# A top-k attention and two expert layers on one core: the order of all instructions settled with other costs and latencies

## The chip, the cores and the metric

The kernel runs on one core of a Trainium2 chip. The metric is the device time of one execution in microseconds (us), taken as the median of repeated runs. Five instruction streams work side by side: TensorE (PE, with its weight loads shown apart as PEld), VectorE (DVE), ScalarE (ACT), GpSimd (POOL) and SyncE (SP), which here issues every DMA.

## What is computed

```python
scores = scale * np.matmul(q, k.transpose(0, 1, 3, 2))          # 4 batches, 8 heads, 576 x 576, head size 64
kth = np.partition(scores, -top_k, axis=-1)[..., -top_k:-top_k + 1]   # top_k = 32
scores = np.where(scores >= kth, scores, -1000000000.0)
scores = scores - np.max(scores, axis=-1, keepdims=True)
attn = np.exp(scores)
attn = attn / (np.sum(attn, axis=-1, keepdims=True) + 1e-09)
x = np.matmul(attn, v)                                          # regrouped to 2304 tokens x 512
h = x @ w_in                                                    # 512 x 2048
x = (h * (1.0 / (1.0 + np.exp(-1.702 * h)))) @ w_out            # 2048 x 512
a = x @ w1; b = x @ w2                                          # 512 x 1024 each
out = ((a * b) @ w3) @ w4                                       # 1024 x 1024, 1024 x 512
```

The weights come as 64-bit floats, q, k and v as 32-bit ones.

## The kernel before

**Numbers.** A 32-bit operand is split into two 16-bit ones, a rounded upper part ("hi") and the rest ("lo"); a product is three matmuls: hi by hi, hi by lo, lo by hi (lines 488, 489, 490, in `product_op`). w3 and w4 are multiplied with each other once ("w34"), so that each token tile needs four products: "h" (w_in), "x2" (w_out), "a" and "b" (w1, w2), "o" (w34). The four weight stores are called win, wout, w12 and w34. While the weights are prepared, free ones of them serve as staging, so the trace shows names such as w<-wout.

**Weight stage.** `load64` brings 128 x 512 numbers of 64 bits by DMA (line 356), three or four passes over ScalarE and GpSimd make pieces of a float (lines 361, 366 or 371, 375), and VectorE joins them (line 379). There are 72 such blocks. A sum of squares over TensorE (line 406) gives one scale for a weight, and `split_op` makes hi and lo of it: hi at lines 313, 330 or 316, lo at 323 (VectorE) or 326 and 327 (GpSimd).

**Attention.** There are 18 tiles of 128 rows, each with 8 heads: 144 heads in all. `head` issues for one of them: S on TensorE (line 706, four or eight matmuls of 128x288); the 32 greatest of 576 on VectorE, four times MAX8 (line 728) with three MATCH_REPLACE8 between (line 731); a bias nb (line 738, GpSimd or VectorE); two passes on ScalarE (746, 749); hi on ScalarE (755), lo on GpSimd (758, 759); a transpose by DMA (762, SP); and the product with v, "av", on TensorE (769, nine or eighteen matmuls). The scores of only two heads fit in PSUM (s_ps).

**Expert layers.** `tile_end` gathers a tile of 8 heads (lines 809, 813, 838), scales it, splits it and transposes it (851). `moe` runs the four products with their splits and transposes between (921 for g, 958 for x2, 1025 for p, the store at 1041). A transposed operand lies in tsb, the operand before in hsb, of which there are three buffers.

**What sets the order.** Nothing is issued as the code is read. Every operation is handed to a planner, class `Order`: with the engines that may take it and a cost in us on each, a due time as priority, the operations it waits for, and the buffers it takes and gives back. `run` then steps through a modelled time. Whenever an engine (T, V, A, G for TensorE, VectorE, ScalarE, GpSimd; D for SP's queue) is free, it takes the ready operation of lowest due time whose buffers are free. An operation becomes ready when the last one it waits for has ended plus a gap: SAME for the same engine, GAP for another. A DMA keeps D for its cost and ends DMA us after that. The order in which operations are taken is the order of instructions on each engine; an operation with several engines goes to the one that takes it first. The chip sees no modelled time, only the order and the semaphores. The due times are set at each call; TensorE's attention work has due - 1000, so that S and av go ahead of products.

```python
u.ready = max(u.ready, o.end + (self.SAME[o.eng] if same else self.GAP))
...
o.end = now + a[1] + (self.DMA if e == "D" else 0.0)
```

Of the kernel before, what the change touches and what calls it, by code (L numbers as in the profile page):

```python
# [35 lines left out]
class Order:  # L36
# [3 lines left out]

    GAP = 0.25
    SAME = {"T": 0.0, "V": 0.11, "A": 0.12, "G": 0.1, "D": 0.25}
    DMA = 2.3

# [7 lines left out]

    def op(self, alts, due, deps=(), env=None, acq=(), rel=(), tag=""):
        o = Op()
        o.alts, o.prio = alts, due
        o.acq = [(a, env, a) if isinstance(a, str) else a for a in acq]
        o.rel = [(a, env, a) if isinstance(a, str) else a for a in rel]
        o.left, o.users, o.ready, o.end, o.why = 0, [], 0.0, None, None
        o.tag, o.seq, o.done = tag, len(self.ops), False
        for d in deps:  # L60
            if d is not None:
                d.users.append(o)
                o.left += 1
        self.ops.append(o)
        return o

    def run(self, log=None):
# [12 lines left out]
        while n < len(self.ops):  # L80
# [18 lines left out]
            for e in engs:  # L99
# [62 lines left out]
def kernel(  # L162
# [126 lines left out]
    def dve_chain(due, fns, deps=(), env=None, acq=(), rel=(), tag=""):  # L289

        o = None
        for i, f in enumerate(fns):
            first, last = i == 0, i == len(fns) - 1
            o = dve(
                0.09, due, f, deps=deps if first else [o], env=env, acq=acq if first else [], rel=rel if last else [], tag=tag
            )
        return o
# [7 lines left out]
    def dma(cost, due, fn, **kw):  # L305
        return op([("D", cost, fn, 0.0)], due, **kw)

    def split_op(due, hi, lo, src, sc, n, deps, env, rel, acq=(), tag="", lo_dve=2.0):
# [22 lines left out]

        o = op([("A", 0.09 + 0.52 * k, f_hi, 0.0), ("G", 0.12 + 0.57 * k, f_hi_g, HI_G), ("V", 0.1 + 0.6 * k, f_hi_v, lo_dve)], due, deps=deps, env=env, acq=acq, tag=tag + "hi")
# [15 lines left out]
    def load64(dst, src, raw_pool, deps):  # L348
# [33 lines left out]

        ld = dma(1.5, due - 20, f_load, deps=deps, env=E, acq=[raw_pool], tag="w load")
        lo = act(0.69, due, f_low, deps=[ld], tag="w low")
        sg = op([("A", 0.55, f_sign_a, 0.0), ("G", 0.9, f_sign, SIGN_G)], due, deps=[lo], tag="w sign")
# [89 lines left out]
    def transpose_op(due, src, acq, dep, env, n=8):  # L475
        def f():
            nc.sync.dma_start_transpose(out=env[acq], in_=src())

        return dma(1.0, due, f, deps=[dep], env=env, acq=[acq], rel=["h"], tag="T")

# [113 lines left out]
    def kv_prep(b, hp, is_v):  # L594
# [53 lines left out]

        kready[b, hp] = [dma(2.0, due, f_t, deps=[m, r], env=E, acq=["kt"], rel=["h", "kr"], tag="k T")]

# [3 lines left out]
    def q_prep(t):  # L654
# [31 lines left out]
        if t == 0:  # L686
            start_prep.append(m)
        tr = dma(1.0, due, f_t, deps=[m], env=E, acq=[("q", E, "qa")], rel=["h"], tag="q T")
        qready[t] = [dma(1.3, due, f_swap, deps=[tr], env=E, acq=[("q", E, "qb")], tag="q swap")]


    def head(t, h, X):
# [87 lines left out]
        if first and j == 0:  # L780
            X["esc", hp] = pool(1.1 * len(pt), due - 6, f_esc(hp, hp + 1), deps=[s], tag="esc")
        elif h == 0:
            o = pool(1.1 * len(pt), due - 6, f_esc(0, NPAIR), deps=[s] + [d for b, _, _, _ in pt for i in range(NPAIR) for d in kready[b, i]], tag="esc")
# [7 lines left out]
        nb = op(  # L791
            [("G", 0.41, f_nb(nc.gpsimd), 0.0), ("V", 0.18, f_nb(nc.vector), NB_DVE)], due - 6, deps=[d, X["esc", hp]],
            env=E, acq=["nb"], tag="nb",
        )
# [24 lines left out]
    def tile_end(t, X):  # L819
# [49 lines left out]
        )  # L869
        X["xt"] = dma(1.0, due, f_t, deps=[s], env=X, acq=["t"], rel=["h"], tag="x T")  # L870


    def hi_lo(due, E, src, deps, rel, acq=(), tag="", wait=2.0, wait_hi=2.0):
# [11 lines left out]
        a = op([("A", 0.52, h_a, 0.0), ("V", 0.42, h_v, wait_hi)], due, deps=deps, env=E, acq=["h"], tag=tag + "hi")  # L885
        return op([("G", 1.18, l(nc.gpsimd), 0.0), ("V", 0.68, l(nc.vector), wait)], due, deps=[a], env=E, rel=rel, tag=tag + "lo")

    def moe(t, X):
# [9 lines left out]
        for j in range(NG):  # L898
# [122 lines left out]
        for j in range(NP_):  # L1021
# [75 lines left out]
```

## Time and profile before

| | us |
|---|---|
| median of three runs (lowest, highest) | 1158.55 (1156.67, 1162.78) |
| the profiled execution, its device time | 1158.71 |
| its span, first to last instruction | 1156.9 |

| engine | busy us | share of the span | instructions |
|---|---|---|---|
| PE | 950.6 | 82% | 5654 |
| DVE | 960.4 | 83% | 2112 |
| ACT | 824.5 | 71% | 1555 |
| POOL | 847.8 | 73% | 1142 |

The profile is of one execution. An engine counts as busy from an instruction's start to its end; consecutive instructions overlap a little, and a matmul's end is modelled, so a busy share is an upper bound of what is used. A wait row names who waited, whom for, and for how long in total. The rows that the prediction uses stand in a section of their own below.

### The profile page before, as it was taken

To read this page: it belongs to the slowest core of one execution; us is meant where nothing else is said; L and a number is where in the kernel's file an instruction comes from. 1 tells how busy PE (TensorE), PEld (TensorE's weight loads), DVE (VectorE), ACT (ScalarE), POOL (GpSimd) and SP (SyncE) were. 2 spreads that over 40 slices of the span, in tenths; PEclk is the share of its full clock that TensorE was granted. 3 is DMA by queue.
4 is the path that set the end of the run, shared out by engine and by line. 5 is a ranking of instruction groups with operands and counts; after the bars stand their busy time and mean duration, and the time that the engine had idled before them with its cause. 6 is when DMAs were issued, how large, how long until landed. Compare 5 with 4: busy or idle time off the path is not lost. (4 is left out here: it accounts for less than half of the span.)

```text
span 1156.9 us, 18481 instructions
## 1 busy us (share of the span) xinstructions
PE 950.6 (82%) x5654; PEld 493.7 (43%) x5654; DVE 960.4 (83%) x2112; ACT 824.5 (71%) x1555; POOL 847.8 (73%) x1142
## 2 busy tenths in 40 slices
PE   2335784556869899999889998989999999999996
PEld 1223342323435445544444544544455455555442
DVE  4887795998999888889898898899999999997311
ACT  6977769768777776877678776767868787776421
POOL 4987796657778878878688886858798787686320
PEclk9999996676979999999899998989999999999998
DMA  8959968466835846677668756666765756657331
GB/s 245 299 134 245 218 163 222 114 150 162 172 56 119 149 103 127 118 143 127 122 116 154 124 113 129 118 110 123 128 136 109 146 110 131 112 96 117 71 59 36
DMA packets 428739, 156.95 MB, mean 136 GB/s; under 512 B 406624, under 2 KB 414816, under 8 KB 428640
## 3 DMA queue, kind: packets, MB, share of 16 engines
q1 hardware_dynamic: 428640, 155.78, 65.0%
q8 instruction: 44, 0.72, 0.3%
q14 instruction: 55, 0.45, 0.1%
HBM read 52.43 MB, written 4.72 MB: 49 GB/s over the span
## 5 line engine op out<-in xcount | busy, mean ns | idle before, releaser
L728 DVE MAX8 m8s<-wsb 128x8 f32<-128x576 f32 x432 | 323.5, 754 | 5.4
L731 DVE MATCH_REPLACE8 wsb<-m8s,wsb 128x576 f32<-128x576 f32 x288 | 213.7, 742 | 0.0
L488 PE MATMUL mm<-w,tsb 128*128 128x512 f16 x432 | 167.9, 389 | 16.4 <-DMA tsb<-hsb 16.3
L488 PEld LDWEIGHTS <-tsb 128*128 128x128 f16 x1072 | 106.5, 99 | 156.6 <-DMA tsb<-hsb 47.1
L759 POOL TENSOR_TENSOR hlb<-ysb,hlb 128x512 f16<-128x512 f32 x144 | 168.1, 1168 | 0.0
L489 PE MATMUL mm<-w,tsb 128*128 128x512 f16 x432 | 167.4, 387 | 0.0
L490 PE MATMUL mm<-w,tsb 128*128 128x512 f16 x432 | 166.7, 386 | 0.0
L490 PEld LDWEIGHTS <-tsb 128*128 128x128 f16 x1072 | 106.7, 100 | 132.6 <-issue 10.6
L769 PE MATMUL av<-v2s,ats 128*128 128x130 f16 (+1 forms) x1440 | 114.1, 235 | 49.5 <-DMA ats<-hlb 40.4
L489 PEld LDWEIGHTS <-tsb 128*128 128x128 f16 x1072 | 106.6, 99 | 110.9 <-issue 13.1
L488 PE MATMUL mm<-wout,tsb 128*128 128x512 f16 x352 | 136.1, 387 | 19.7 <-DMA tsb<-hsb 16.7
L728 DVE MAX8 m8s<-s_ps 128x8 f32<-128x576 f32 x144 | 108.8, 756 | 47.4 <-PE s_ps L706 38.9
L746 ACT ACTIVATE s_ps<-s_ps,m8s 128x576 f32<-128x576 f32 x144 | 102.4, 711 | 54.7 <-DVE m8s L728 45.8
L749 ACT ACTIVATE ysb<-s_ps,nbs,asm 128x576 f32<-128x576 f32 x144 | 119.6, 831 | 28.3 <-DVE nbs L738 13.5
L490 PE MATMUL mm<-wout,tsb 128*128 128x512 f16 x352 | 136.0, 386 | 0.0
L489 PE MATMUL mm<-wout,tsb 128*128 128x512 f16 x352 | 135.9, 386 | 0.0
L769 PEld LDWEIGHTS <-ats 128*128 128x128 f16 (+1 forms) x1440 | 97.3, 108 | 82.9 <-DMA ats<-hlb 53.2
L706 PE MATMUL s_ps<-kts,qts 128*128 128x288 f16 (+1 forms) x640 | 106.8, 312 | 30.8 <-ACT ysb L749 24.7
L488 PE MATMUL mm<-win,tsb 128*128 128x512 f16 x288 | 112.4, 390 | 5.6 <-DMA tsb<-hsb 3.1
L489 PE MATMUL mm<-win,tsb 128*128 128x512 f16 x288 | 112.0, 389 | 0.0
L490 PE MATMUL mm<-win,tsb 128*128 128x512 f16 x288 | 111.8, 388 | 0.0
L918 POOL TENSOR_TENSOR fsb<-fsb 128x512 f32<-128x512 f32 x68 | 88.2, 1298 | 29.4 <-ACT fsb L909 27.1
(194 smaller groups left out, 1877.4 us busy)
## 6 DMA issues: line engine op xcount, KB each, us to landing
w<-in_moe_w_dram SPq DMA_DIRECT2D x16, 512.0 KB, 5.3
wout<-in_moe_w_in_dram SPq DMA_DIRECT2D x16, 512.0 KB, 5.3
wout<-in_moe_w_out_dram SPq DMA_DIRECT2D x16, 512.0 KB, 4.7
qts<-qts SPq DMA_DIRECT2D x36, 128.0 KB, 2.6
out_dram<-fsb SPq DMA_DIRECT2D x18, 256.0 KB, 2.4
w<-in_moe_w_out_dram SPq DMA_DIRECT2D x8, 512.0 KB, 5.0
psb<-in_moe_w_dram SPq DMA_DIRECT2D x8, 512.0 KB, 4.6
tsb<-in_moe_w_dram SPq DMA_DIRECT2D x8, 512.0 KB, 5.1
```

Of the source, the lines that this page charges most:

```text
L488: nc.tensor.matmul(o, a[:, i, :], hi, start=(first and i == 0), stop=False)
L489: nc.tensor.matmul(o, a[:, i, :], lo, start=False, stop=False)
L490: nc.tensor.matmul(o, a[:, 4 + i, :], hi, start=False, stop=(last and i == 3))
L706: nc.tensor.matmul(E["sp"][r : r + n, i], qe[q_][:, h, r : r + n], kt[:, j, i * HS : (i + 1) * HS], start=k_ == 0, stop=k_ == 1,)
L728: nc.vector.max(out=E["m8"][:, 8 * i : 8 * i + 8], in_=E["sp"] if i == 0 else E["w"])
L731: nc.vector.match_replace(out=two(E["w"]) if i == 0 else E["w"], in_to_replace=E["m8"][:, 8 * i : 8 * i + 8], in_values=E["sp"] if i == 0 ...
L746: nc.scalar.activation(E["sp"], E["sp"], AF.Prelu, bias=E["m8"][:, TOPK - 1 : TOPK], scale=-1.0, alpha=1.0 / FAR)
L749: nc.scalar.activation(two(E["y"]), E["sp"], AF.Exp, bias=E["nb"], scale=nesc)
L759: nc.gpsimd.tensor_tensor(hl()[:, S + SR : 2 * S], E["y"][:, 0:SM], hl()[:, 0:SM], op=ALU.subtract)
L769: nc.tensor.matmul(X["av", hp][r : r + n, j], E["at"][:, i, r : r + n], v2[:, j, blk, :], start=(i == 0), stop=(i == 8))
L918: nc.gpsimd.tensor_tensor(E["f"], E["f"], E["f2"], op=ALU.mult)
```

## The change

Only the numbers that the planner works with are changed; no operation is added or taken away, and no due time. The one gap of 0.25 us to another engine becomes five, by the engine that ends. A DMA's time after its issue becomes 2.1 us for all and can be set for one operation (`lat`); the weight loads have 3.6. A transpose's time on SP goes from 1.0 (1.1 for a head's) to 1.32 (1.35), the three transposes of a k operand together from 2.0 to 3.9. Some thirty costs of operations are set anew, most by under 0.2 us. The diff, cut to these:

```diff
-    GAP = 0.25
+    GAP = {"T": 0.25, "V": 0.16, "A": 0.16, "G": 0.1, "D": 0.05}
     SAME = {"T": 0.0, "V": 0.11, "A": 0.12, "G": 0.1, "D": 0.25}
-    DMA = 2.3
+    DMA = 2.1
...
-                    u.ready = max(u.ready, o.end + (self.SAME[o.eng] if same else self.GAP))
+                    u.ready = max(u.ready, o.end + (self.SAME[o.eng] if same else self.GAP[o.eng]))
...
-                o.end = now + a[1] + (self.DMA if e == "D" else 0.0)
+                o.end = now + a[1] + ((self.DMA if o.lat is None else o.lat) if e == "D" else 0.0)
                 for name, env, key in o.rel:
-                    t = o.end + self.GAP
+                    t = o.end + self.GAP[e]
...
-        alts = [("V", 0.1 + 0.9 * k, f_lo_v, lo_dve)]
+        alts = [("V", 0.1 + (1.0 if tag == "w " else 0.6) * k, f_lo_v, lo_dve)]
         if lo_dve > 0.0:
-            alts.append(("G", 0.4 + 1.5 * k, f_lo_g, 0.0))
+            alts.append(("G", 0.5 + (2.0 if tag == "w " else 1.4) * k, f_lo_g, 0.0))
...
-        ld = dma(1.5, due - 20, f_load, deps=deps, env=E, acq=[raw_pool], tag="w load")
+        ld = dma(1.3, due - 20, f_load, deps=deps, env=E, acq=[raw_pool], tag="w load", lat=3.6)
...
-        return dve(0.87, due, f_join, deps=[sg, mn], env=E, rel=[raw_pool], tag="w join")
+        return dve(0.72, due, f_join, deps=[sg, mn], env=E, rel=[raw_pool], tag="w join")
...
-        kready[b, hp] = [dma(2.0, due, f_t, deps=[m, r], env=E, acq=["kt"], rel=["h", "kr"], tag="k T")]
+        kready[b, hp] = [dma(3.9, due, f_t, deps=[m, r], env=E, acq=["kt"], rel=["h", "kr"], tag="k T")]
...
-        lo = pool(1.5, due + 7, f_lo, deps=[hi], env=E, rel=["y"], tag="a lo")
-        tr = dma(1.1, due + 8, f_t, deps=[lo], env=E, acq=["at"], rel=["hl"], tag="a T")
+        lo = pool(1.42, due + 7, f_lo, deps=[hi], env=E, rel=["y"], tag="a lo")
+        tr = dma(1.35, due + 8, f_t, deps=[lo], env=E, acq=["at"], rel=["hl"], tag="a T")
...
-            gs.append((E, dma(1.0, due, f_t, deps=[lo], env=E, acq=["t"], rel=["h"], tag="g T")))
+            gs.append((E, dma(1.32, due, f_t, deps=[lo], env=E, acq=["t"], rel=["h"], tag="g T")))
```

**Two places in the new order.** On VectorE, in the weight stage, where blocks of w_out are joined (L379: the staging buffers lie in wout, the store is w_70, that is w12; L728 and L731 are attention). Before:

```order
L379 SCALAR_TENSOR_TENSOR w_70<-wout,w_70 128x512
L728 MAX m8s<-wsb 128x8
L738 TENSOR_SCALAR nbs<-m8s,asm 128x1
L379 SCALAR_TENSOR_TENSOR w_70<-wout,w_70 128x512 x3
L728 MAX m8s<-s_ps_95 128x8
L731 MATCH_REPLACE wsb<-m8s,s_ps_95 128x576
L379 SCALAR_TENSOR_TENSOR w_70<-wout,w_70 128x512
L728 MAX m8s<-wsb 128x8
L731 MATCH_REPLACE wsb<-m8s,wsb 128x576
L379 SCALAR_TENSOR_TENSOR w_70<-wout,w_70 128x512
L728 MAX m8s<-wsb 128x8
L731 MATCH_REPLACE wsb<-m8s,wsb 128x576
```

With the change:

```order
L379 SCALAR_TENSOR_TENSOR w_70<-wout,w_70 128x512
L728 MAX m8s<-wsb 128x8
L728 MAX m8s<-s_ps_95 128x8
L731 MATCH_REPLACE wsb<-m8s,s_ps_95 128x576
L728 MAX m8s<-wsb 128x8
L379 SCALAR_TENSOR_TENSOR w_70<-wout,w_70 128x512
L731 MATCH_REPLACE wsb<-m8s,wsb 128x576
L728 MAX m8s<-wsb 128x8
L731 MATCH_REPLACE wsb<-m8s,wsb 128x576
L379 SCALAR_TENSOR_TENSOR w_70<-wout,w_70 128x512 x2
L813 TENSOR_TENSOR xsb<-xsb,av 128x2x64
L728 MAX m8s<-wsb 128x8
```

Six joins with seven attention instructions became four joins with eight. Counted over the whole stage, the last of the 72 joins stands behind 97 MAX8 (24.25 heads) before and behind 113 (28.25 heads) with the change; the 40th behind 40 and 43.

On SP, at the end, the transposes of the last tile's attention output (L851) and of the next to last tile's g (L921); L762 is the last head's. Before:

```order
L762 DMA_TRANSPOSE ats<-hlb 128x9x128
L1025 DMA_TRANSPOSE tsb<-hsb 128x8x128 x2
L921 DMA_TRANSPOSE tsb<-hsb 128x8x128
L851 DMA_TRANSPOSE tsb<-hsb 128x8x128
L921 DMA_TRANSPOSE tsb<-hsb 128x8x128
L1041 DMA out_dram<-fsb 128x512
```

And with the change:

```order
L762 DMA_TRANSPOSE ats<-hlb 128x9x128 x2
L1025 DMA_TRANSPOSE tsb<-hsb 128x8x128 x2
L851 DMA_TRANSPOSE tsb<-hsb 128x8x128
L921 DMA_TRANSPOSE tsb<-hsb 128x8x128 x2
L1041 DMA out_dram<-fsb 128x512
```

The last tile's transpose has moved ahead of both of the g transposes.

## Rows read from the trace of the kernel before

**Rows 1.** Busy time by stage: us, then PE, PEld, DVE, ACT, POOL; PEclk, DMA share, GB/s.
```profile
0.00:150.00 150.00, 71.07 (x440) 40.65 (x441) 111.29 (x234) 117.01 (x218) 112.40 (x146) 0.99 0.89 223
150.00:350.00 200.00, 127.74 (x686) 65.82 (x685) 179.11 (x343) 152.83 (x275) 148.57 (x170) 0.75 0.62 149
350.00:800.00 450.00, 416.18 (x2530) 217.19 (x2529) 401.00 (x931) 326.18 (x637) 359.26 (x510) 0.97 0.66 125
800.00:1062.00 262.00, 254.13 (x1627) 133.97 (x1626) 251.19 (x569) 199.05 (x371) 204.40 (x290) 1.00 0.65 122
1062.00:1157.00 95.00, 81.49 (x377) 36.10 (x375) 17.80 (x39) 29.44 (x57) 23.14 (x29) 0.96 0.32 59
```

**Rows 2.** Waits of PE, 350 to 800 us: us in total, times, longest.
```profile
PE mm L488 <- DMA tsb<-hsb: 13.9, 12, 2.2
PE s_ps L706 <- ACT ysb L749: 8.9, 8, 4.1
PE av L769 <- DMA ats<-hlb: 2.8, 2, 2.4
```

**Rows 3.** Waits of DVE, 350 to 800 us.
```profile
DVE m8s L728 <- PE s_ps L706: 28.8, 22, 3.8
```

**Rows 4.** Waits of DVE, 0 to 350 us, its joins: longest and shortest of four.
```profile
DVE w L379 <- ACT wout L375: 10.7, 7, 2.9
...
DVE w L379 <- ACT tsb L375: 2.4, 2, 2.2
```

**Rows 5.** Waits of ACT, 0 to 350 us, for weights: first and last of three.
```profile
ACT w L361 <- DMA wout<-in_moe_w_in_dram: 10.4, 8, 3.0
...
ACT w L361 <- DMA wout<-in_moe_w_out_dram: 4.3, 4, 3.0
```

**Rows 6.** DMA issues: count, KB each, median us from issue to landing.
```profile
w<-in_moe_w_dram SPq DMA_DIRECT2D x16, 512.0 KB, 5.3
...
wout<-in_moe_w_out_dram SPq DMA_DIRECT2D x16, 512.0 KB, 4.7
...
ats<-hlb SPq DMA_TRANSPOSE x144, 3.3
```

**Rows 7.** A head's transpose on SP (line 762): ns min/median/max, first and last start.
```profile
L762 SPq DMA_TRANSPOSE ats<-hlb x144: 1241/1303/4777, 46.0 to 1066.5; - x144
```

**Rows 8.** Groups by shape: busy us, mean ns, idle before.
```profile
L323 DVE SCALAR_TENSOR_TENSOR wout<-w,wsm,wout 128x512 f16<-128x512 f32 x10 | 13.2, 1386 | 0.0
L323 DVE SCALAR_TENSOR_TENSOR wout<-wout,wsm 128x512 f16<-128x512 f32 x2 | 1.6, 784 | 0.0
L451 DVE TENSOR_SCALAR fsb<-w,wsm 128x512 f32<-128x512 f32 x11 | 7.9, 723 | 0.0
L738 DVE TENSOR_SCALAR nbs<-m8s,asm 128x1 f32<-128x1 f32 x64 | 16.7, 262 | 0.7
L755 ACT CAST hlb<-ysb 128x576 f16<-128x576 f32 x144 | 97.2, 676 | 6.8 <-DMA ats<-hlb 5.2
L759 POOL TENSOR_TENSOR hlb<-ysb,hlb 128x512 f16<-128x512 f32 x144 | 168.1, 1168 | 0.0
```

**Rows 9.** The joins of line 379: ns min/median/max.
```profile
L379 DVE SCALAR_TENSOR_TENSOR win<-w,win x16: 668/858/1684, 41.9 to 80.8; 128x512 uint32<-128x512 uint32 x16
```

**Rows 10.** Timeline: start, us, instruction; a product's first and third matmul.
```profile
1013.09 0.38 PE L488 MATMUL mm<-win,tsb 128*128 128x512 f16 x1
...
1013.52 0.38 PE L490 MATMUL mm<-win,tsb 128*128 128x512 f16 x1
```

**Rows 11.** Timeline of ACT and SP at the end.
```profile
1072.19 0.26 ACT L809 COPY xsb<-av 128x130 f32<-128x130 f32 x1
...
1079.81 0.63 ACT L843 ACTIVATE hsb<-xsb 128x512 f16<-128x512 f32 x1 [4.04 <-DMA tsb<-hsb]
...
1082.36 1.23 SPq L851 DMA_TRANSPOSE tsb<-hsb  x1
```

**Rows 12.** Line 728 (MAX8) up to 384 us: DVE busy and count; PEclk, DMA share, GB/s.
```profile
0.00:384.00 384.00, 103.20 (x140) 0.87 0.73 177
```

More of the change, by code (lines that the diff above doesn't have):

```diff
@@ L51, in pool, with op @@
         self.pools[name] = [(0.0, -1 - i, s) for i, s in enumerate(slots)]
-    def op(self, alts, due, deps=(), env=None, acq=(), rel=(), tag=""):
+    def op(self, alts, due, deps=(), env=None, acq=(), rel=(), tag="", lat=None):
         o = Op()
-        o.alts, o.prio = alts, due
+        o.alts, o.prio, o.lat = alts, due, lat
         o.acq = [(a, env, a) if isinstance(a, str) else a for a in acq]
@@ L294, in dve_chain @@
             o = dve(
-                0.09, due, f, deps=deps if first else [o], env=env, acq=acq if first else [], rel=rel if last else [], tag=tag
+                0.12, due, f, deps=deps if first else [o], env=env, acq=acq if first else [], rel=rel if last else [], tag=tag
             )
@@ L381, in f_join @@
             )
[L383 to L385 removed]
+        ld = dma(1.3, due - 20, f_load, deps=deps, env=E, acq=[raw_pool], tag="w load", lat=3.6)
+        lo = act(0.65, due, f_low, deps=[ld], tag="w low")
+        sg = op([("A", 0.63, f_sign_a, 0.0), ("G", 0.75, f_sign, SIGN_G)], due, deps=[lo], tag="w sign")
         mn = act(0.57, due, f_main, deps=[ld, sg], tag="w main")
[L387 removed]
+        return dve(0.72, due, f_join, deps=[sg, mn], env=E, rel=[raw_pool], tag="w join")
     ncol = [0]
@@ L477, in f @@
             nc.sync.dma_start_transpose(out=env[acq], in_=src())
-        return dma(1.0, due, f, deps=[dep], env=env, acq=[acq], rel=["h"], tag="T")
+        return dma(1.32, due, f, deps=[dep], env=env, acq=[acq], rel=["h"], tag="T")
     def product_op(due, get, at, w, blocks, first, last, deps, acq, rel, tag):
@@ L687, in q_prep @@
             start_prep.append(m)
-        tr = dma(1.0, due, f_t, deps=[m], env=E, acq=[("q", E, "qa")], rel=["h"], tag="q T")
-        qready[t] = [dma(1.3, due, f_swap, deps=[tr], env=E, acq=[("q", E, "qb")], tag="q swap")]
+        tr = dma(1.32, due, f_t, deps=[m], env=E, acq=[("q", E, "qa")], rel=["h"], tag="q T")
+        qready[t] = [dma(1.5, due, f_swap, deps=[tr], env=E, acq=[("q", E, "qb")], tag="q swap")]
     def head(t, h, X):
@@ L780, in head @@
         if first and j == 0:
-            X["esc", hp] = pool(1.1 * len(pt), due - 6, f_esc(hp, hp + 1), deps=[s], tag="esc")
+            X["esc", hp] = pool(0.87 * len(pt), due - 6, f_esc(hp, hp + 1), deps=[s], tag="esc")
         elif h == 0:
-            o = pool(1.1 * len(pt), due - 6, f_esc(0, NPAIR), deps=[s] + [d for b, _, _, _ in pt for i in range(NPAIR) for d in kready[b, i]], tag="esc")
+            o = pool(0.87 * len(pt), due - 6, f_esc(0, NPAIR), deps=[s] + [d for b, _, _, _ in pt for i in range(NPAIR) for d in kready[b, i]], tag="esc")
             for i in range(NPAIR):
@@ L791, in head @@
         nb = op(
-            [("G", 0.41, f_nb(nc.gpsimd), 0.0), ("V", 0.18, f_nb(nc.vector), NB_DVE)], due - 6, deps=[d, X["esc", hp]],
+            [("G", 0.34, f_nb(nc.gpsimd), 0.0), ("V", 0.18, f_nb(nc.vector), NB_DVE)], due - 6, deps=[d, X["esc", hp]],
             env=E, acq=["nb"], tag="nb",
@@ L869, in tile_end @@
         )
-        X["xt"] = dma(1.0, due, f_t, deps=[s], env=X, acq=["t"], rel=["h"], tag="x T")
+        X["xt"] = dma(1.32, due, f_t, deps=[s], env=X, acq=["t"], rel=["h"], tag="x T")
     def hi_lo(due, E, src, deps, rel, acq=(), tag="", wait=2.0, wait_hi=2.0):
@@ L885, in hi_lo @@
         a = op([("A", 0.52, h_a, 0.0), ("V", 0.42, h_v, wait_hi)], due, deps=deps, env=E, acq=["h"], tag=tag + "hi")
-        return op([("G", 1.18, l(nc.gpsimd), 0.0), ("V", 0.68, l(nc.vector), wait)], due, deps=[a], env=E, rel=rel, tag=tag + "lo")
+        return op([("G", 1.13, l(nc.gpsimd), 0.0), ("V", 0.68, l(nc.vector), wait)], due, deps=[a], env=E, rel=rel, tag=tag + "lo")
     def moe(t, X):
@@ L966, in moe @@
         lo = dve(0.66, due, f_lo, deps=[hi], env=x2e, rel=["mm"], tag="x2 lo")
-        x2t = dma(1.0, due, f_t2, deps=[lo], env=x2e, acq=["x2t"], rel=["h"], tag="x2 T")
+        x2t = dma(1.32, due, f_t2, deps=[lo], env=x2e, acq=["x2t"], rel=["h"], tag="x2 T")
         sgo = pool(0.34, due, f_sg, deps=[c, ready["c"]], tag="sg")
@@ L1030, in moe @@
             )
-            tr = dma(1.0, due, f_t, deps=[lo], env=E, acq=["pt"], rel=["h"], tag="p T")
+            tr = dma(1.32, due, f_t, deps=[lo], env=E, acq=["pt"], rel=["h"], tag="p T")
             pr = product_op(
```

4 lines of the change are left out of this document (2 added, 2 removed).

## The prediction

> **What bounds the kernel now.** I read the busy time by stage first, since the share over the whole span hides that the bound changes [rows 1]. Up to 150 us all engines work, none above 117 of 150: transfers and chains of weight pieces. From 150 to 350 VectorE leads with 179 of 200; TensorE has little to do (128 of 200) and a granted clock of 0.75, a mean of stretches at 1.2 and at 2.4 GHz. From 350 to 800 TensorE and VectorE are level, 416 and 401 of 450, so 34 and 49 us are idle. From 800 to 1062 both are nearly full, 254 and 251 of 262. Behind 1062 attention is over and TensorE empties its backlog, 81 of 95. Two things follow. An order that only moves work inside 800 to 1062 can win some 8 us. What can be won lies in the waits ahead of 800, and it counts only if TensorE gets its work earlier too.
>
> Then the waits. In the middle stage TensorE waits 13.9 us in 12 pieces for transposed operands of products, 8.9 for a free score buffer, 2.8 for a head's transpose [rows 2], and VectorE 28.8 us for scores, which stand behind those in TensorE's queue [rows 3]. In the weight stage VectorE stands 26.1 us in 22 pieces, by four such rows, in front of joins [rows 4], whose pieces ScalarE made late, itself waiting 19.4 us in 16 pieces, by three rows, for loads [rows 5].
>
> **How true the planner's numbers were.** The change adds and removes no instruction; it is worth what the planner got wrong. A weight load was planned at 1.5 + 2.3 = 3.8 us and takes 4.7 to 5.3 [rows 6]; it becomes 1.3 + 3.6 = 4.9. A transpose kept SP for 1.0 or 1.1 and in truth keeps it for 1.30 [rows 7]; it becomes 1.32 or 1.35. Its whole time was 3.3 to 3.4 without the gap, and 3.3 is measured [rows 6], so what was wrong is how soon the next one on SP can go. Other costs move by a tenth and mostly towards the trace.
>
> **The terms.** The sum starts at the profiled execution's 1158.7, which lies 0.2 above the median of the runs.
>
> 1. *Choice of engines.* An operation with two engines may change sides. Counted in the two orders, VectorE takes seven more second halves of weight splits (three at 0.78, four near 1.39: 7.9), and five more pieces of k, v, q and g (at most 0.72 or so each: 3.4). It gives up nine other weight pieces, each near 0.72, and eight nb at 0.26 [rows 8]: 6.5 + 2.1. That is +2.7 for VectorE, nearly all ahead of 350, where VectorE leads. GpSimd gets about the opposite and has a quarter of its time free [rows 1]. **+3**, between 0, if other work hides it, and +6, if what it gives up was hidden.
>
> 2. *Weight stage.* The last join moves behind four more heads (24.25 to 28.25), most of it between the 40th and the 56th join (10 to 10.75 and 14.25 to 17.5): the first of the two places shown. So attention fills the time in which a load is on its way. The 22 waits average 1.2 us, and the load's plan was short by 0.9 to 1.5: the error has the size of the waits. All of it would be -26. But attention fits only where scores are there, and ScalarE and GpSimd, which make the pieces, stay as they are. I take **-10**, with -26 and 0 as ends; a loss here is a rival below.
>
> 3. *Middle stage.* With SP's true 1.3 us a product is placed where its transpose has landed. Of the 13.9 us I take more than half, **-8**; the far end is all of TensorE's three waits, -26. The other end is a loss. From the end of a head's exponential to its av the old plan had 0.58 + 1.5 + 1.1 + 2.3 and three gaps of 0.25, 6.23; the new has 0.58 + 1.42 + 1.35 + 2.1 and gaps of 0.16, 0.1 and 0.05, 5.76. The trace has 0.68 on ScalarE, 1.17 and a smaller one on GpSimd [rows 8] and 3.3 [rows 6], 5.2 without the small one and any gap. The slack of half a microsecond is gone, and a late av holds up what is behind it. If each second of the 70 heads in this stage waits 0.3, that is +10.
>
> 4. *Late stage.* Nearly full on both engines: 0, between -8 and +4.
>
> 5. *The end.* Behind the last S stand 130 blocks of three matmuls before and 122 after. Matmuls start 0.215 us apart (0.43 from the first to the third) [rows 10], so a block is 0.65 and the backlog is 5.2 us smaller; those blocks went ahead of the last S, where TensorE is as full, so 0. The last tile's x now has its transpose ahead of both g transposes, the second of the places. Between the last av and the first product with x stand 14 blocks, 9.1 us, and before 22, 14.2. From the last av's copy at 1072.19 to the issue at 1082.36 are 10.2 us, 4.04 of them a wait for one of three hsb buffers, whose third a g held [rows 11]; that g now comes later, so 6.1 + 3.3 for the landing [rows 6] is 9.4 against 9.1. **+0.3**. If the buffer is not free, 4 more.
>
> The sum is 1158.7 + 3 - 10 - 8 + 0.3 = **1144.0**.
>
> **A rule weighed.** The joins' cost in the plan goes from 0.87 to 0.72. The trace has 0.67 at best, 0.86 in the middle and 1.68 at worst for one group of them [rows 9], so the new number is that of a join that meets nothing. The Trainium skill (SBUF — State Buffer, "SBUF: two separate sides") says that a VectorE instruction with two SBUF inputs and a GpSimd instruction take a shared port pair as an exclusive lock, the loser waiting for the whole instruction. The spread of one and the same join agrees with it. By that rule a plan with single numbers for joins stays wrong however it is measured, and this speaks against the change.
> From rows alone: 72 joins at 0.86 in place of 0.72 put VectorE up to 10 us behind plan, or 0 where a join's end lies beside the next instruction's start. Behind plan, VectorE keeps the staging buffers longer and SP stands in front of the next load. This belongs to rival C.
>
> **The rivals.**
>
> *A: it goes as above*, waits shrink in the weight and the middle stage, 1144; with the far ends of terms 2 and 3, 1158.7 + 3 - 26 - 26 = 1110, which I hold for very unlikely as both engines are then full throughout.
>
> *B: the waits change their place.* Products wait less, av and scores more, since the slack of a head's chain is gone (+10 of term 3 in place of -8), and the weight stage gives its 10: 1158.7 + 3 - 10 + 10, and 4 less for products that do wait less, is 1158. For it speaks that VectorE's greatest wait is for scores [rows 3], whose release by the exponential has no better cost than before (0.73 both times). Against it, that av waits only 2.8 us in this stage now [rows 2].
>
> *C: slower, weights too late for TensorE.* The 160th S matmul (head 36) stands near 385 us, as 140 MAX8 or 35 heads have started by 384 [rows 12]. It has 190 product blocks ahead of it before and 174 with the change; by the 208th (head 44) both have 240. So TensorE reaches head 36 with 16 blocks or 10.4 us less done. Ahead of that TensorE has idle time, behind it little [rows 1], so what is missing there is added at the end, unless head 36 comes that much earlier. If the waits in front of joins stay, and VectorE is 3 behind for its extra work: 1158.7 + 10.4 + 3 = 1172. The point that decides is the time of the 140th MAX8: at 375 or earlier A, at 384 or later C. For it speaks the clock of 0.75 in that stretch, at which TensorE catches up slowly [rows 1].
> The Trainium skill (TensorE: Matmul & The Clock Gate, "HAM oscillation") says that a TensorE that waits falls back to half clock; the row of 0.75 agrees, and by that rule fewer waits would give back more than their own length.
>
> *D: the order differs, the time does not,* since 800 to 1157 is full anyway. This is B's case for the result.
>
> **How the numbers follow.** A measurement of this kernel can tell about 0.5%, 5.8 us, from no change; so faster is under 1152.8 and slower over 1164.3. A has 0.54: the two largest corrections have the size and the place of the two largest removable waits. B and D together 0.22. C and the like 0.24: a list order reacts to small changes by chance as well, and both engines being full leaves little to give. The range is from 1121, two thirds of A's way to its far ends, to 1172, which is C; I leave out about one in ten on either side.
>
> **What would show it.** Right: VectorE's waits in front of line 379 under 18 us; products waiting for tsb under 7 us between 350 and 800; the 140th MAX8 by 375 us; hardly a wait for hsb at line 843 of the last tile. Wrong: av waiting for ats over 10 us in the middle stage (B); the 140th MAX8 no earlier than 384 and TensorE as full as now behind it (C).

## The result, and the profile after

The changed kernel takes 1125.88 us in the median of four runs (1125.77 to 1127.88), the kernel before 1157.61 in four runs beside it (1156.63 to 1162.78). The ratio is 0.972, with a 95% interval from 0.969 to 0.975: 31.7 us faster. The prediction had the direction and its range held the time, but of the 31.7 us it had forecast 14.6.

The stages first: us, then PE, PEld, DVE, ACT, POOL, then PEclk, DMA share and GB/s, as in [rows 1].

```profile
0.00:150.00 150.00, 76.05 (x467) 42.47 (x468) 124.41 (x258) 118.34 (x220) 113.13 (x151) 0.94 0.88 228
150.00:350.00 200.00, 131.64 (x727) 69.31 (x726) 180.62 (x348) 157.49 (x283) 148.00 (x169) 0.76 0.63 151
350.00:800.00 450.00, 432.73 (x2673) 225.46 (x2671) 424.20 (x976) 345.69 (x675) 374.71 (x538) 0.99 0.69 131
```

Between 350 and 800 us TensorE's idle time fell from 34 to 17 us and VectorE's from 49 to 26; TensorE runs 2673 matmul records there in place of 2530. Up to 150 us VectorE does 13 us more, from 150 to 350 only 1.5 more. The granted clock of 0.75 in the second stage stays (0.76), so none of the gain came from there. Over a whole run the granted clock was 0.942, 0.924, 0.950 and 0.927 in the four runs of the changed kernel, whose times lie within 2.1 us.

The MAX8 of line 728, up to two times; after, then before:

```profile
0.00:365.00 365.00, 103.25 (x140) 0.85 0.73 182
0.00:800.00 800.00, 312.47 (x421) 0.92 0.71 154
```
```profile
0.00:834.00 834.00, 311.96 (x421) 0.92 0.70 149
```

The score matmuls of line 706, with the first and the last start; before, then after:

```profile
L706 PE MATMUL s_ps<-kts,qts x640: 282/286/448, 18.7 to 1053.9; 128*128 128x288 f16 x128, 128*64 128x288 f16 x32
```
```profile
L706 PE MATMUL s_ps<-kts,qts x640: 282/286/448, 17.6 to 1028.0; 128*128 128x288 f16 x128, 128*64 128x288 f16 x32
```

The 140th MAX8 (head 35) has started by 365 us, before by 384 [rows 12]: 19 us lead. The 421st (head 105) has by 800, before by 834: 34 us lead. So more than half of the gain was there at head 35, and the middle stage gave 15 us more. At the last score matmul the lead is 26, at the end of the two profiled executions 32.7 (spans of 1156.9 and 1124.2): 8 us are lost ahead of the last scores and 7 come back behind them.

Waits of TensorE, 350 to 800 us: us in total, times, longest.

```profile
PE s_ps L706 <- ACT ysb L749: 6.3, 7, 2.2
PE mm L488 <- DMA tsb<-hsb: 5.6, 5, 2.0
PE av L769 <- DMA ats<-hlb: 3.9, 4, 1.7
PE av L769 <- DVE xsb L813: 0.9, 1, 0.9
```

Before, three more rows with over 0.5 us stood beside those of [rows 2]:

```profile
PE av L769 <- DVE xsb L813: 4.2, 2, 2.1
...
PE av L769 <- POOL v2s L327: 2.1, 1, 2.1
PE mm L627 <- ACT v2s L623: 0.7, 1, 0.7
```

All of TensorE's waits in this stage together were 32.8 us and are 16.7.

Of VectorE in the same stretch:

```profile
DVE m8s L728 <- PE s_ps L706: 12.5, 16, 1.4
```

And of VectorE, 0 to 350 us, in front of its joins:

```profile
DVE wout L379 <- ACT w L375: 9.6, 5, 3.6
DVE w L379 <- ACT wout L375: 6.4, 4, 2.4
...
DVE win L379 <- ACT w L375: 0.9, 2, 0.6
```

Products wait 5.6 us for transposed operands, 13.9 before; a free score buffer takes 6.3, 8.9 before; a head's transpose 3.9, 2.8 before [rows 2]. VectorE's wait for scores fell most, from 28.8 to 12.5 [rows 3]. Joins wait 16.9 by three rows, 26.1 before [rows 4]. But from 150 to 350 us, where joins wait 3.9 less (9.7 before, 5.8 after), scores make VectorE wait 3.7 longer; before, then after:

```profile
DVE m8s L728 <- PE s_ps L706: 6.5, 4, 4.6
```
```profile
DVE m8s L728 <- PE s_ps L706: 10.2, 6, 4.7
```

Every sign that I had named as "right" came.

The end, on ScalarE, SP and TensorE, beside [rows 11]:

```profile
1042.80 0.27 ACT L809 COPY xsb<-av 128x130 f32<-128x130 f32 x1 [0.19 <-PE av L769]
1044.90 0.63 ACT L843 ACTIVATE hsb<-xsb 128x512 f16<-128x512 f32 x1 [1.83 <-DVE xsb L838]
...
1048.16 1.23 SPq L851 DMA_TRANSPOSE tsb<-hsb  x1
...
1053.66 0.39 PE L488 MATMUL mm<-wout,tsb 128*128 128x512 f16 x1 [0.49 <-DMA tsb<-hsb]
```

From the last av's copy to the issue of the last tile's transpose are 5.4 us, 10.2 before; the wait of 4.04 for a buffer is gone.

### The profile page after: what moved, and what is told of

The parts are those of the page before. It is cut to its first block, busy times and chain, and to the rows that moved or that the text cites. A ratio compares the mean times of both kernels' runs of the same rounds, so it can differ in the third digit from the quotient of the medians.

```text
span 1124.2 us, 18486 instructions
## 1 busy us (share of the span) xinstructions
PE 941.6 (84%) x5654; PEld 488.4 (43%) x5654; DVE 967.4 (86%) x2107; ACT 821.6 (73%) x1550; POOL 843.0 (75%) x1145
## 4 chain that ended last, share of the span: by engine, by line
PE 38%; DVE 26%; POOL 12%; DMA 10%; ACT 7%; issue 6%; SPq 1%; POOLq 0%; ACTq 0%; DVEq 0%
PE mm L488 10%; DVE m8s L728 10%; PE mm L490 10%; PE mm L489 10%; DVE wsb L731 8%; DMA tsb<-hsb 6%; PE av L769 3%; PE s_ps L706 3%; DMA ats<-hlb 3%; POOL hsb L327 2%; POOL hlb L759 2%; DVE wout L323 2%; POOL hsb L883 1%; POOL fsb L918 1%; ACT ysb L749 1%
## 5 line engine op out<-in xcount | busy, mean ns | idle before, releaser
L728 DVE MAX8 m8s<-wsb 128x8 f32<-128x576 f32 x432 | 324.4, 756 | 6.2
L731 DVE MATCH_REPLACE8 wsb<-m8s,wsb 128x576 f32<-128x576 f32 x288 | 213.8, 743 | 0.0
L488 PE MATMUL mm<-w,tsb 128*128 128x512 f16 x432 | 166.3, 385 | 13.1 <-DMA tsb<-hsb 12.5
L728 DVE MAX8 m8s<-s_ps 128x8 f32<-128x576 f32 x144 | 108.9, 756 | 36.2 <-PE s_ps L706 31.6
L769 PE MATMUL av<-v2s,ats 128*128 128x130 f16 (+1 forms) x1440 | 111.0, 231 | 23.4 <-DMA ats<-hlb 20.2
L769 PEld LDWEIGHTS <-ats 128*128 128x128 f16 (+1 forms) x1440 | 94.3, 105 | 55.7 <-DMA ats<-hlb 30.2
L731 DVE MATCH_REPLACE8 wsb<-m8s,s_ps 128x576 f32<-128x576 f32 x144 | 107.6, 748 | 0.0
```

The costliest lines, as they stand in the source:

```text
L488: nc.tensor.matmul(o, a[:, i, :], hi, start=(first and i == 0), stop=False)
L728: nc.vector.max(out=E["m8"][:, 8 * i : 8 * i + 8], in_=E["sp"] if i == 0 else E["w"])
L731: nc.vector.match_replace(out=two(E["w"]) if i == 0 else E["w"], in_to_replace=E["m8"][:, 8 * i : 8 * i + 8], in_values=E["sp"] if i == 0 ...
L769: nc.tensor.matmul(X["av", hp][r : r + n, j], E["at"][:, i, r : r + n], v2[:, j, blk, :], start=(i == 0), stop=(i == 8))
```

## The experiments

A planner's table can't be tried piece by piece in the hope that pieces add up: each number changes the whole order. So I sorted the changed numbers into three groups, built all their combinations, and then built the same plan again with a number changed that means nothing (a draw, in what follows). All eighteen kernels are the same operations in another order, some of them on the other of their two engines. Each ran once, in five batches, each on another chip; the kernel before, run beside each batch, took 1158.9, 1161.3, 1155.0, 1159.7 and 1154.2, so a difference under some 7 us between two kernels is not read.

My theory was that of the prediction: the load latency gives the weight stage's gain, the true time of a product's transpose the middle stage's. The rivals: the gain is one group's alone, or only chance.

**1. Each group alone in the plan of before.** b_lat has the gaps, a DMA's time and the load; b_sp has all of SP's times; b_dur has the compute costs.

```diff
# b_lat
-    GAP = 0.25
+    GAP = {"T": 0.25, "V": 0.16, "A": 0.16, "G": 0.1, "D": 0.05}
-    DMA = 2.3
+    DMA = 2.1
-        ld = dma(1.5, due - 20, f_load, deps=deps, env=E, acq=[raw_pool], tag="w load")
+        ld = dma(1.3, due - 20, f_load, deps=deps, env=E, acq=[raw_pool], tag="w load", lat=3.6)
# b_sp
-        return dma(1.0, due, f, deps=[dep], env=env, acq=[acq], rel=["h"], tag="T")
+        return dma(1.32, due, f, deps=[dep], env=env, acq=[acq], rel=["h"], tag="T")
-        kready[b, hp] = [dma(2.0, due, f_t, deps=[m, r], env=E, acq=["kt"], rel=["h", "kr"], tag="k T")]
+        kready[b, hp] = [dma(3.9, due, f_t, deps=[m, r], env=E, acq=["kt"], rel=["h", "kr"], tag="k T")]
...
# b_dur
-        return dve(0.87, due, f_join, deps=[sg, mn], env=E, rel=[raw_pool], tag="w join")
+        return dve(0.72, due, f_join, deps=[sg, mn], env=E, rel=[raw_pool], tag="w join")
...
```

b_lat. Expected: 

> The kernel before with the latencies of the change alone: the five gaps, 2.1 us for a DMA after its issue, and the weight load's 1.3 + 3.6. T: the weight stage's gain, the 140th MAX8 near 366 in place of 384 us, the middle stage's waits of VectorE for scores stay near 29; 1140. L: 1125 to 1175, with no tie to a stage.

b_sp. Expected: 

> The kernel before with the transposes' time on SP alone (1.32 and 1.35, 3.9 for the three of a k operand, 1.5 for the swap of q). T: the middle stage's gain: VectorE's wait for scores from 350 to 800 near 13 in place of 29 us, products waiting for tsb near 6 in place of 14; the 140th MAX8 stays at 384; 1142. L: 1125 to 1175, with no tie to a stage.

b_dur. Expected: 

> The kernel before with the costs of computing operations alone (pieces and joins of weights, splits, lo, nb, esc, g, the chains on VectorE); SP's costs and all latencies as before. Theory S (SP's time is what counts, as it keeps transposes from being planned faster than SP can issue them; a tiny change of a number alone moves the time by 10): 1150 to 1175. Rival D (true durations matter as much): 1130 to 1145. Rival L (chance alone): anything from 1130 to 1190.

Measured: b_lat 1187.6, b_sp 1142.2, b_dur 1157.9. The true load latency, with the new gaps, made the kernel 29 us *slower* than the kernel before beside it; SP's times alone brought half of the gain. b_sp hit its time, but none of the signs that went with it: VectorE waits 32.3 us for scores (expected near 13), products 10.6 for tsb (near 6), and the 140th MAX8 has started by 358 us (384). So this hit is luck. In b_lat the 140th MAX8 comes at 390, not at 366. Part 3 shows how little one run of one plan says.

**2. Each group taken out of the changed plan,** which is also each pair of groups in the plan of before: a_nosp (SP's times as before), a_nolat (gaps, DMA and load as before), b_latsp (compute costs as before).

```diff
# a_nosp
-        return dma(1.32, due, f, deps=[dep], env=env, acq=[acq], rel=["h"], tag="T")
+        return dma(1.0, due, f, deps=[dep], env=env, acq=[acq], rel=["h"], tag="T")
-        kready[b, hp] = [dma(3.9, due, f_t, deps=[m, r], env=E, acq=["kt"], rel=["h", "kr"], tag="k T")]
+        kready[b, hp] = [dma(2.0, due, f_t, deps=[m, r], env=E, acq=["kt"], rel=["h", "kr"], tag="k T")]
...
# a_nolat
-    DMA = 2.1
+    DMA = 2.3
...
# b_latsp
-        return dve(0.72, due, f_join, deps=[sg, mn], env=E, rel=[raw_pool], tag="w join")
+        return dve(0.87, due, f_join, deps=[sg, mn], env=E, rel=[raw_pool], tag="w join")
...
```

a_nosp. Expected: 

> The changed kernel with SP's costs put back (1.0, 1.1, 2.0 and 1.3); latencies and durations as changed, so that a transpose is planned 0.3 short in all. S: the gain is lost and more, 1165 to 1195, as with the latencies alone. D: half of the gain stays, 1140. L: anything from 1130 to 1190.

a_nolat. Expected: 

> The changed kernel with the latencies put back (one gap of 0.25, 2.3 us for a DMA after its issue, the load 1.5); SP's costs and durations as changed. S: the gain stays for the most part, 1125 to 1150. D: the same. A theory in which the load's latency gives the weight stage its gain, the one of the prediction: the 140th MAX8 back near 384, 1145 to 1155. L: anything from 1130 to 1190.

b_latsp. Expected: 

> The kernel before with latencies and SP's costs of the change, durations as before. S: 1125 to 1150; a transpose in all is as true as in the changed kernel. D: 1140 to 1155. L: anything from 1130 to 1190.

Measured: 1177.9, 1141.6, 1152.3. SP's times are worth 15 us in the plan of before (1158 to 1142), 35 beside the latencies (1188 to 1152), 16 beside the compute costs (1158 to 1142) and 52 beside both (1178 to 1126): a gain each time, 30 in the mean. The latencies cost 30 us in the plan of before and 20 beside the compute costs, where SP's times are false; where these are true they cost 10 without the compute costs and bring 16 with them. In a_nolat the 140th MAX8 has started by 376 us, between the 384 that the theory of the prediction had said and the 365 of the changed kernel.

**3. The same plans drawn again.** A DMA's time moves by 0.03 us, which means nothing: b_jit is the plan of before, a_jit and a_jit2 the changed one.

```diff
# b_jit
-    DMA = 2.3
+    DMA = 2.33
# a_jit
-    DMA = 2.1
+    DMA = 2.13
# a_jit2
-    DMA = 2.1
+    DMA = 2.07
```

b_jit. Expected: 

> The kernel before with one planner number moved by next to nothing: the time of a DMA after its issue 2.33 us in place of 2.3. No number becomes truer. Theory T (the time follows how true the planner's numbers are): within 6 us of 1157.6. Rival L (every new order draws its time by chance, and the change drew a good one): any place from 1125 to 1175, more than 6 us off.

a_jit. Expected: 

> The changed kernel with the time of a DMA after its issue 2.13 us in place of 2.1. T: within 6 us of 1125.9. L: as a chance order, most likely slower by 6 to 40 us, since 1125.9 was a good draw.

a_jit2. Expected: 

> The changed kernel with 2.07 us in place of 2.1 behind an issue; a second sample of what a change of next to nothing does. From the first two (10 us each, both slower): between 1126 and 1140. If the change were a lucky draw by more than that: 1140 to 1160.

Measured: 1169.3, 1136.7 and 1144.8. A number without meaning moves the time by 11 to 19 us here, and by 30, 6 and 9 in the draws of part 5 (a_nokt13 and a_nokt07 beside a_nokt, b_kt33 beside b_kt). So no single pair of plans proves a cause, and that holds for each pair of parts 1, 2 and 4 that differs by some 30 us or less. Part of the 31.7 can be a good draw. All of it is not: the three draws of the changed plan have a mean of 1135.8 and the two of the plan before 1163.5, 27.7 apart, and none of the three is as slow as either of the two.

**4. SP's time with the landing kept.** a_occ10 lets SP go as early as the old plan did, but lets the transpose land when the new one does; a_occ16 keeps SP for longer than it is kept.

```diff
# a_occ10
-        return dma(1.32, due, f, deps=[dep], env=env, acq=[acq], rel=["h"], tag="T")
+        return dma(1, due, f, deps=[dep], env=env, acq=[acq], rel=["h"], tag="T", lat=2.42)
...
# a_occ16
-        return dma(1.32, due, f, deps=[dep], env=env, acq=[acq], rel=["h"], tag="T")
+        return dma(1.6, due, f, deps=[dep], env=env, acq=[acq], rel=["h"], tag="T", lat=1.82)
...
```

a_occ10. Expected: 

> The changed kernel with SP's own costs as before (1.0, 1.1, 2.0, 1.3) and what is taken from them put behind the issue (2.42 in place of 2.1 and so on), so that each transpose lands at the planned time as in the change, and only SP is planned free too early. Theory Q (what counts is SP's occupancy): 1160 to 1180, as with SP's costs put back (1177.9). Theory E (what counts is the whole time from issue to landing): 1126 to 1145. L (chance): no tie.

a_occ16. Expected: 

> The changed kernel with SP's costs raised over the truth by 0.28 (1.6, 1.63, 4.7, 1.8) and the same taken from the time behind the issue, so the whole time stays. Q with truth best: 1130 to 1150, a little slower than 1125.9. A variant of Q, in which room on SP is what helps and more is better: under 1120. E: 1126 to 1140.

Measured: 1163.1 and 1142.4. With the right landing and SP free too early the whole gain is gone in this draw; with SP kept too long about half of it stays (15 of 31.7). As far as one draw of each can tell, it is SP's occupancy that the plan has to know, more than the landing.

**5. The k operand by itself.** a_nokt is the changed plan with only the k operand's three transposes (and q's swap) at their old times; a_nokt13 and a_nokt07 are the same with the two draws of part 3. a_ktonly has all other transposes old and the k operand new. b_kt and b_kt33 are the plan of before, in both its draws, with one number changed.

```diff
# a_nokt (a_nokt13, a_nokt07: also DMA = 2.13, DMA = 2.07)
-        kready[b, hp] = [dma(3.9, due, f_t, deps=[m, r], env=E, acq=["kt"], rel=["h", "kr"], tag="k T")]
+        kready[b, hp] = [dma(2.0, due, f_t, deps=[m, r], env=E, acq=["kt"], rel=["h", "kr"], tag="k T")]
-        qready[t] = [dma(1.5, due, f_swap, deps=[tr], env=E, acq=[("q", E, "qb")], tag="q swap")]
+        qready[t] = [dma(1.3, due, f_swap, deps=[tr], env=E, acq=[("q", E, "qb")], tag="q swap")]
# a_ktonly
-        tr = dma(1.35, due + 8, f_t, deps=[lo], env=E, acq=["at"], rel=["hl"], tag="a T")
+        tr = dma(1.1, due + 8, f_t, deps=[lo], env=E, acq=["at"], rel=["hl"], tag="a T")
...
# b_kt (b_kt33: also DMA = 2.33)
-        kready[b, hp] = [dma(2.0, due, f_t, deps=[m, r], env=E, acq=["kt"], rel=["h", "kr"], tag="k T")]
+        kready[b, hp] = [dma(3.9, due, f_t, deps=[m, r], env=E, acq=["kt"], rel=["h", "kr"], tag="k T")]
```

a_nokt. Expected: 

> The changed kernel with the three transposes of a k operand back at 2.0 and the swap at 1.3; all other transposes at 1.32 and 1.35. There are 16 of the former and 322 of the latter. If the many count: 1126 to 1145. If the 16, which lie in front of a batch's scores, count: 1160 or more.

a_nokt13. Expected: 

> The changed plan with the k operand's three transposes back at 2.0 on SP and the swap at 1.3, as in the earlier run that took 1167.8, and a DMA's time at 2.13 in place of 2.1, a change without meaning that draws another order; the full plan at 2.13 took 1136.7. Theory K (what is lost is the planner's knowledge that a k operand keeps SP for 3.9): slower than 1136.7 by over 15, so above 1152. Rival J (the 1167.8 was a bad draw): within 10 of 1136.7, so 1127 to 1147.

a_nokt07. Expected: 

> The same with a DMA's time at 2.07; the full plan at 2.07 took 1144.8. Theory K: above 1158. Rival J: 1135 to 1155. Both runs of this pair on one side decide between K and J; one on each side leaves it open.

a_ktonly. Expected: 

> The changed plan with all transposes of products, heads, q and x back at 1.0 and 1.1 on SP, but the k operand kept at 3.9 and the swap at 1.5; with all of SP's costs old the plan took 1177.9, with all new 1125.9. If the k operand carries SP's whole part: below 1145. If both kinds of transposes are needed: 1150 to 1165. If the k operand is nothing: near 1178, above 1168.

b_kt. Expected: 

> The plan of before with one number changed, the k operand's transposes from 2.0 to 3.9 on SP. If that alone brings what all of SP's costs brought in the plan of before (1142.2): 1136 to 1148. If it works only together with the other costs: 1152 to 1165, as before. Above 1165: a true number alone in a false plan does harm, as the latencies alone did.

b_kt33. Expected: 

> The plan of before with the k operand's transposes at 3.9 and a DMA's time at 2.33 in place of 2.3, the same change without meaning as in the plan of before that took 1169.3. With 2.3 the k operand's number alone brought 23.5. If the k operand's true time is a gain in itself: 1135 to 1157, over 12 below 1169.3. If 1136.3 was a good draw: 1160 to 1175.

Measured, as pairs that differ by the k operand's time (in the first four also by the swap's, 1.3 or 1.5):

| pair | 2.0 for the k operand | 3.9 | gain |
|---|---|---|---|
| a_nokt, the changed kernel | 1167.8 | 1125.9 | 41.9 |
| a_nokt13, a_jit | 1138.3 | 1136.7 | 1.7 |
| a_nokt07, a_jit2 | 1161.9 | 1144.8 | 17.1 |
| a_nosp, a_ktonly | 1177.9 | 1162.0 | 15.9 |
| the kernel before, b_kt | 1157.6 | 1136.3 | 21.3 |
| b_jit, b_kt33 | 1169.3 | 1144.9 | 24.4 |

Five gains, and one of 1.7 that can't be told from nothing; 20.4 in the mean, which by the scatter of the six is good to some 14 either way (95%). a_nokt13 took the time of rival J and a_nokt07 that of theory K, which by what was said beforehand left it open; b_kt and b_kt33, which differ from their partners by this number alone, then came out as the theory says. Taken as plans with all their draws, the means are 1163.5 (before) and 1140.6 (before with 3.9), 1156.0 (changed with 2.0) and 1135.8 (changed). So one number of the plan, 2.0 to 3.9, brings 20 to 23 of the 27.7 us, in the plan of before as well, and all else in the change 5 to 7.

Whether the other 322 transposes count beside it stays open. a_ktonly, where only they are false, took 1162.0, the time that was said to mean "both kinds are needed", 36 us over the changed kernel; but in the plan of before their true times beside the k operand's (b_sp, 1142.2) brought nothing over the k operand's alone (b_kt, 1136.3). Each of these is one draw.

How the number can cost time, the trace of a_nosp shows at one place, an example and no proof. SP, GpSimd (the lo of a head, which its transpose waits for) and TensorE: start, us, instruction.

```profile
583.04 2.54 SPq L644 DMA_TRANSPOSE kts<-hsb  x2
585.63 1.23 SPq L647 DMA_TRANSPOSE kts<-kr  x1
586.97 1.30 SPq L762 DMA_TRANSPOSE ats<-hlb  x1
...
584.01 1.16 POOL L759 TENSOR_TENSOR hlb<-ysb,hlb 128x512 f16<-128x512 f32 x1
...
590.22 0.70 PE L769 MATMUL av<-v2s,ats 128*128 128x130 f16 x9 [0.58 <-DMA ats<-hlb]
590.76 0.65 PE L706 MATMUL s_ps<-kts,qts 128*128 128x288 f16 x4
```

The three transposes keep SP from 583.04 to 586.86, 3.8 us (in the kernel before 3.87 in the median of all 16 operands). By the plan's 2.0 it would be free at 585.04, about when the head's lo is done (585.17); the transpose goes at 586.97, 1.8 later. av then waits at the head of TensorE's queue, 0.58 us here, and the next scores stand behind it. In the kernel before, a head's transpose starts within 0.5 us of such a triple's end 8 times in 16, with the change twice; over the nine plans with 2.0 it is 6.0 in the mean, over the eleven with 3.9 it is 3.4.

TensorE's waits for a head's transpose, 350 to 800, in a_nokt, b_lat and b_kt:

```profile
PE av L769 <- DMA ats<-hlb: 9.7, 10, 2.0
```
```profile
PE av L769 <- DMA ats<-hlb: 17.3, 15, 3.7
```
```profile
PE av L769 <- DMA ats<-hlb: 5.5, 6, 2.4
```

This path isn't the whole of it. In the kernel before av waits only 2.8 us; there the k operand's number (b_kt) takes the products' wait for tsb from 13.9 to 6.2 and lets av's rise to 5.5, while in the other draw (b_jit to b_kt33) products go from 7.9 to 12.8 and av from 12.3 to 6.2. What falls in all six pairs is the sum of TensorE's waits from 350 to 800 us, by 13.5, 0.3, 9.6, 7.1, 9.9 and 8.2 us in the order of the table. Which wait takes the loss differs from draw to draw, and the way from the number to the waits is not shown.

**6. The join's cost,** the number against which I had weighed a rule.

```diff
-        return dve(0.72, due, f_join, deps=[sg, mn], env=E, rel=[raw_pool], tag="w join")
+        return dve(0.86, due, f_join, deps=[sg, mn], env=E, rel=[raw_pool], tag="w join")
```

a_join. Expected: 

> The changed plan with the cost of a weight join at 0.86, near the mean of a join that meets a held port, in place of 0.72, which is that of one that meets nothing. If the joins' too low cost puts the weight stage behind its plan, as the rule on the shared port would have it: at or below 1126, with the 140th MAX8 before 366 us. If it is one more draw of the changed plan: 1126 to 1150, as the two others (1136.7 and 1144.8).

Measured: 1123.2, the least of all, but inside what a draw moves, and not by way of the weight stage: by 366 us it has 138 MAX8, two fewer than the changed kernel. It gains in the middle stage, where VectorE hardly waits for scores any more:

```profile
DVE m8s L728 <- PE s_ps L706: 4.8, 5, 1.5
```

As one execution it is no proof of a better version.

**All plans together.** MAX8 started by 350 us; MAX8 from 350 to 800; all waits of TensorE, 350 to 800 (us); av's wait for ats among them; and the waits of all joins on ScalarE's last piece, 0 to 350 (us).

| plan | us | to 350 | 350 to 800 | TensorE | av | joins |
|---|---|---|---|---|---|---|
| *k operand at 2.0* | | | | | | |
| before | 1157.6 | 117 | 280 | 32.8 | 2.8 | 26.6 |
| b_jit | 1169.3 | 121 | 278 | 35.2 | 12.3 | 26.1 |
| b_lat | 1187.6 | 116 | 274 | 33.8 | 17.3 | 24.5 |
| b_dur | 1157.9 | 119 | 283 | 28.5 | 10.1 | 19.7 |
| a_nosp | 1177.9 | 117 | 277 | 34.8 | 9.0 | 13.5 |
| a_occ10 | 1163.1 | 123 | 283 | 27.5 | 12.1 | 13.8 |
| a_nokt | 1167.8 | 120 | 283 | 30.2 | 9.7 | 15.9 |
| a_nokt13 | 1138.3 | 123 | 289 | 25.0 | 9.0 | 17.3 |
| a_nokt07 | 1161.9 | 124 | 281 | 32.3 | 9.5 | 12.0 |
| *k operand at 3.9 (a_occ16: 4.7)* | | | | | | |
| b_sp | 1142.2 | 134 | 276 | 28.8 | 3.8 | 29.1 |
| b_latsp | 1152.3 | 123 | 285 | 28.2 | 5.8 | 24.3 |
| b_kt | 1136.3 | 123 | 292 | 22.9 | 5.5 | 34.5 |
| b_kt33 | 1144.9 | 118 | 291 | 27.0 | 6.2 | 22.7 |
| a_nolat | 1141.6 | 122 | 288 | 27.7 | 4.2 | 19.6 |
| a_ktonly | 1162.0 | 126 | 286 | 27.7 | 6.9 | 14.2 |
| a_occ16 | 1142.4 | 125 | 293 | 20.7 | 2.5 | 19.3 |
| a_jit | 1136.7 | 130 | 287 | 24.7 | 4.6 | 16.0 |
| a_jit2 | 1144.8 | 122 | 292 | 22.7 | 5.3 | 22.8 |
| after | 1125.9 | 129 | 292 | 16.7 | 3.9 | 17.3 |
| a_join | 1123.2 | 127 | 297 | 15.6 | 2.5 | 20.6 |

The means are 1164.6 and 1141.1, 23.5 apart, with one plan of each group on the other's side (a_nokt13, a_ktonly). av waits 9 us or more in all of the upper group but the kernel before, and under 7 in all of the lower. Over the twenty plans the time goes with all of TensorE's waits (correlation 0.87) and with av's (0.79), but neither with the products' wait for tsb (-0.01) nor with the joins' (-0.17). Measured from these means, the 31.7 us are 23.5 between the groups, plus 15.2 by which the changed kernel lies below its own group, less the 7.0 by which the kernel before lies below its own. The groups hold the other edits unevenly, so this is a way to see the size of a draw, not a second measurement.

## Why the prediction was right or wrong

**Term 1 (choice of engines, +3).** VectorE is busy for 967.4 us in place of 960.4, 7.0 more where the term had counted 2.7. What that costs was not tried alone.

**Term 2 (weight stage, -10) came out larger, 19 us at head 35, and its reason was wrong.** The step that failed is "the error has the size of the waits": that the load's short plan made VectorE wait in front of joins, and that attention would fill that time. The term had this between the 40th and the 56th join, which in the kernel before start at 139 and 212 us; but VectorE's idle time fell by 13 us ahead of 150 us, where joins give 5 of it, and by 1.5 from 150 to 350, where scores took what joins gave. In the table the joins' wait runs from 12.0 to 34.5 us with next to no relation to the time: a_nosp has 13.5 and takes 1177.9, b_kt has 34.5 and takes 1136.3. With the true load latency alone (b_lat) heads come no earlier (116 MAX8 by 350 us, before 117). My sign "joins wait under 18" came without the cause that it was to show: a_nosp shows it too, and is slower than before. SP's times alone (b_sp) brought the greatest lead there, 134. But the changed plan's lead is partly a draw: a_jit2, the same plan but for 0.03 us, has 122, and the k operand alone does little here (b_kt 123, b_kt33 118, beside 117 and 121). Which of SP's other times carries the lead in b_sp was not tried.

**Term 3 (middle stage, -8) had the right resource, SP's time, and left out the number that weighs most; it is the term that was mis-sized.** By the lead, 34 us at head 105 and 19 at head 35, it measured -15. The prediction priced a transpose's 1.0 to 1.32, a third of a microsecond each, and its wait of 13.9 us. It never priced the k operand, whose 2.0 became 3.9 in the same diff: 1.9 us at a time by which SP ran behind its plan, sixteen times. In the two pairs that differ by this number alone it brought 12 and 13 MAX8 more between 350 and 800 us (b_kt 292 beside 280, b_kt33 291 beside 278): three heads, at 450 / (280 / 4) = 6.4 us a head some 20 us, of gains of 21 and 24. Over the groups 350 to 800 us holds 281 and 289 MAX8 in the mean; b_sp, with 276, doesn't follow.

The wait that the term did price fell by what it was priced at, 13.9 to 5.6, and makes half of the 16 us that TensorE waits less in this stage. But over the plans it doesn't go with the time: b_kt33 has 12.8 and takes 1144.9, a_ktonly has 3.7 and takes 1162.0. So that agreement says little for the reason.

The other end of term 3, that the slack of a head's chain is gone (6.23 to 5.76 in the plan), is seen where the latencies are new and SP's times old: av waits 17.3 us and the kernel loses 29 (b_lat, one draw). That is rival B. In the changed kernel av waits 3.9, as it waits under 7 in all plans with the k operand at 3.9.

**Term 4 (late, 0) and term 5 (the end, +0.3) were right as a sum**, -1 against the 34 us of lead at head 105: the lead is 32.7 at the end. Of the 8 us lost ahead of the last scores and the 7 won behind them, 5.2 are the eight blocks fewer that term 5 had counted behind the last S and set off against each other. The transpose of x comes 5.4 us after the copy, the buffer is free, and TensorE waits 0.49 us for a g transpose (its product is with w_out), and for none ahead of a product with w_in, which is what x goes to.

**Rival C** rested on the 140th MAX8. It came at 365, before the 375 that I had set, so the blocks that were moved behind head 36 cost nothing that shows. The granted clock between 150 and 350 us did not change (0.75, 0.76), so fewer waits there gave nothing back through the clock. Nor do the rows tie the clock to waits alone: up to 150 us TensorE is busy for 71 of 150 us at a granted clock of 0.99 [rows 1]. **The rule weighed** on the joins' cost changed nothing that can be told from a draw (a_join).

What the forecast lacked beside the k operand is a measure of chance. "A list order reacts to small changes by chance as well" stood in it with no number. The number is 6 to 30 us for 0.03 us of planned time, as large as each of my terms.

## What to carry to other kernels

In a static order, price every number of the diff, and look at how far a single operation puts its queue behind plan, not only at the sum. Here 322 transposes at 0.25 to 0.32 us add up to some 93 us and sixteen k operands at 1.9 to 30, and it was the sixteen that were seen to bring a gain in both plans; that it is the size of the single error that counts is my reading and was not tried. A plan seems to need the time that a queue is kept more than the time at which a transfer lands: true latencies in a plan with false occupancies made things worse twice out of twice (by 30 and 20 us, one draw each). And before a difference of two orders is given a cause, draw each again with a number that means nothing; where the time moves by as much, compare groups of plans, not pairs.

## What was not expected of the hardware

Three transposes in a row of one k operand keep SP for 3.87 us in the median (of 16, by the starts and ends in the trace of the kernel before), and up to 5.4, where each by itself has a median near 1.2 to 1.3:

```profile
L644 SPq DMA_TRANSPOSE kts<-hsb x32: 1189/1257/2167, 13.6 to 856.3; - x32
...
L647 SPq DMA_TRANSPOSE kts<-kr x16: 1174/1205/1978, 16.2 to 857.6; - x16
```

So a queue's time adds up by the instruction, 2 x 1.26 + 1.21 = 3.7 and a little between them.
